# One exponential per score bank with the fp16 half copied from SBUF, and PSUM banks moved from scores to row maxima

## The chip, the cores and the metric

The kernel runs on one core of a Trainium2 chip. The metric is the device time of one execution in microseconds, from three runs of the kernel; lower is better. The engines are named as in the profile: PE (TensorE matmuls; PEld are its weight loads), DVE (VectorE), ACT (ScalarE), POOL (GpSimd) and SP (SyncE, which issues most DMAs).

## The reference

Two parts follow each other. First clustered attention: 2 batches, 8 heads, 768 tokens, head size 64. Each query and key is assigned to the nearest of 16 normalised centroids of its head, and only pairs of the same cluster may see each other:

```python
mask = q_assign[:, :, :, None] == k_assign[:, :, None, :]
scores = scale * np.matmul(q, k.transpose(0, 1, 3, 2))
scores = np.where(mask, scores, -1000000000.0)
scores = scores - np.max(scores, axis=-1, keepdims=True)
attn = np.exp(scores)
attn = attn / (np.sum(attn, axis=-1, keepdims=True) + 1e-09)
return np.matmul(attn, v).astype(np.float32)
```

Its result, as 1536 tokens of 512 values, goes through two feed-forward layers (512 to 2048 to 512), each `g(x @ w_in) @ w_out`. The first has a quadratic piece between -1 and 1 and the identity above, the second is `s * relu(h)**2 + b`. The weights arrive as float64 and are converted on the chip.

## The kernel before

The program is one hand-written order of instructions for each engine, and each engine runs its own in order. Precision comes from splitting: a number is held as a high part and a low part, and a product is three matmuls (high by high, high by low, low by high).

**Attention** is a loop over 96 slots, six for each of the 16 heads; a slot `t` handles 128 keys against all 768 queries of a head, the 768 in two halves of 384, one PSUM bank each. `slot(t)` emits, in this order: `max_mm(u, 0)` for a slot nine later (`LEAD = 9`); the DMAs planned for the slot; `scores(t)`, two matmuls into each of two banks "s"; `max_mm(u, 1)`; `finish` of a head that ended (DVE reads the bank "o"); the PE, ACT and DVE parts of planned steps; `max_reduce(u)`, two reductions on DVE that read the two banks "m"; `probs(t)`; and `values(t - 2)` (`LAG = 2`), 18 small matmuls that take `ph` and `pl` as weights and accumulate into the single bank "o".

`probs(t)` makes from each half of the scores an fp16 exponential `ph` and an fp32 exponential `pf` of the same numbers, two ACT instructions per half (L823, L824). POOL then takes the difference `pl = pf - ph` (L826; DVE does it in two slots). `pf` has two buffers, `ph` and `pl` three each.

**PSUM** has eight banks, given out from four pools, each of which hands out its banks in turn: "s" has 3, "m" 2, "o" 1, "x" 2. A pool hands a bank to its next user, and that user's first write waits until every reader of the bank's last user has finished. `spare()` takes a bank of the kind that stands next in the list `spares`, or of "x" if the list is empty.

Planned work lies between: transposes of q and k (L491, their high halves taken out of PSUM by ACT at L504), cluster assignment (L544, L583), the scaling of v (`split_v`, two ACT instructions of L673 for each pair of heads), the row that carries a head's maximum (`max_row`, L791 and a DMA `qb<-mr`), and `x_out`, the transposes of a finished pair of heads (L884), which ACT and DVE read at L889 and L892.

**Feed-forward** is 96 units. `ff_step(n)` emits `emit_h` of unit `n` (12 matmuls into one bank "h"), then `ff_rest(n)` (ACT, DVE and POOL work: the activation of unit `n`, the split of unit `n - 1`, the conversion of coming weights), then `emit_y` of unit `n - 2` (12 matmuls into four banks "y", taken from "m", "x", "o", "m"). In the first layer the bank of `h` is read last by L268 on DVE, and the conversions of weights (four DVE instructions each, L151 to L163) stand ahead of it in DVE's order. The bank of `h` comes from the pool "s".

The two parts overlap at the seam: unit 0 runs in slots 91 to 94, in a bank "m", unit 1 in slots 96 and 97, in a bank "s". From slot 98 on `spares` holds "s", so that the two `x_out` of the last pair take banks of that pool too, and the order on PE from there is: y of unit 0, `x_out(7, 0)`, h of unit 2, `x_out(7, 1)`, h of unit 3, y of unit 1, h of unit 4, y of unit 2.

```python
        for n in range(2):
            at(extra, NS + 3 + n, lambda n: whole(x_out(NP - 1, n)), n)
...
        at(extra, NS + 2, spares.append, "s")
...
        for n in range(2, TAIL):
            at(extra, NS + n + 1, emit_h, *units[n])
            at(extra, NS + n + 1, ff_rest, n)
```

Of the kernel before, what the change touches and what calls it, by code (L numbers as in the profile page):

```python
# [13 lines left out]
ACTF = mybir.ActivationFunctionType  # L14
# [11 lines left out]
def clustered_attention_moe_kernel(  # L26
# [24 lines left out]
    nc = tc.nc  # L51
# [16 lines left out]
    qk_scale = 1.0 / float(D) ** 0.5  # L68
# [26 lines left out]

    banks = {
        x: ctx.enter_context(tc.tile_pool(name="ps_" + x, bufs=n, space=PSUM))
        for x, n in (("s", 3), ("m", 2), ("o", 1), ("x", 2))
    }

    def bank(kind, name):
# [305 lines left out]
    def attention(es, prep):  # L407
# [35 lines left out]
        spares = []  # L443
# [324 lines left out]
        def max_first(i, fill):  # L768


            hd = heads[i]
            m2 = smp.tile([128, J, 2], F32, tag="rowmax2", name="rowmax2", bufs=2)
            for j in range(J):
                for n in range(2):
                    ps = spare()[:, 0:S // 2]
                    nc.tensor.matmul(
                        ps, lhsT=hd["qb"][0:NQ, j * 128:(j + 1) * 128],
                        rhs=hd["kb"][0:NQ, n * S // 2:(n + 1) * S // 2], start=True, stop=True,
                    )
                    if fill:  # L780
                        f, a, k = fill.pop(0)
                        f(*a, **k)
                    nc.vector.tensor_reduce(out=m2[:, j, n:n + 1], in_=ps, axis=AX.X, op=ALU.max)
            max_end(i, m2)
# [33 lines left out]
        def probs(t):  # L818
            pf = pp.tile([128, S], F32, tag="pf", name="pf")
            ph = phl.tile([128, S], F16, tag="ph", name="ph")  # L820
            pl = phl.tile([128, S], F16, tag="pl", name="pl")
            for qs, ps in pr[t]:
                nc.scalar.activation(out=ph[:, qs], in_=ps, func=ACTF.Exp, scale=qk_scale)  # L823
                nc.scalar.activation(out=pf[:, qs], in_=ps, func=ACTF.Exp, scale=qk_scale)  # L824
            eng = nc.vector if t in VPL else nc.gpsimd
            eng.tensor_tensor(out=pl, in0=pf, in1=ph, op=ALU.subtract)  # L826
            pr[t] = (ph, pl)
# [191 lines left out]
        def slot(t):  # L1019
            x = steps.get(t - 1, ())  # L1020
            u = t + LEAD
            has_max = 0 <= u < NS
            if has_max:
                max_mm(u, 0)
            for f, a in dmas.get(t, ()):
                f(*a)
            if 0 <= t < NS:
                scores(t)
            if has_max:
                max_mm(u, 1)  # L1030
            d = t - 1 - LAG
            if 0 <= d < NS and d % J == J - 1:
                finish(d // J)
            run(x, 3)
            if has_max:
                max_reduce(u)
            run(x, 1)
            if 0 <= t < NS:
                probs(t)
            run(x, 2)  # L1040
            for f, a in mid.get(t, ()):
                f(*a)
            if 0 <= t - LAG < NS:
                values(t - LAG)
            run(steps.get(t, ()), 0)
            for f, a in extra.get(t, ()):
                f(*a)
# [71 lines left out]
        for x in (s0, s1):  # L1119
# [5 lines left out]
            out=eye[:, 2:4], in0=ident[0:2, 0:2], scalar1=2.0 ** -14 / S, scalar2=None, op0=ALU.mult  # L1125
# [25 lines left out]
        for a in range(2):  # L1151
            for t in range(2):
                for x in sims1:
                    x[0](((a, t),), fill)
        spares[:] = ["s", "m", "s", "m", "s"]
        max_first(0, fill)
        spares[:] = ["o"]
        whole(max_row(0))
# [24 lines left out]
    with tc.manual_schedule():  # L1183
        with ExitStack() as es, ExitStack() as prep:
            attention(es, prep)
        ff_pools(("wc", NWC))
        for n in range(TAIL, len(units) + 2):
            ff_step(n)
# [33 lines left out]
```

## Time and profile before

| what | value |
|---|---|
| median of 3 runs | 767.8 us (767.29 to 767.82) |
| span of the profiled execution, first to last instruction | 766.2 us |
| PE busy, all of the span | 747.7 us (98%) |
| ACT busy | 472.9 us (62%) |
| DVE busy | 483.3 us (63%) |
| POOL busy | 318.3 us (42%) |
| mean granted TensorE clock | 0.997 of full |

The profile is of one execution and gives no total time of its own, only the span; the median of the runs is 1.6 us above that span, and what is said of microseconds of the span is carried over to the runs as it stands. PE is busy nearly throughout, so its few idle stretches are what waits show; the other engines are near their limits only in the attention loop and shortly after it.

### The profile page before, as it was taken

What the parts mean: (1) busy time and instruction counts of PE and PEld (TensorE: products, weight loads), DVE (VectorE), ACT (ScalarE), POOL (GpSimd) and SP (SyncE); (2) the same over time, 40 slices, a digit from 0 to 9 for tenths busy, and PEclk for the clock granted to TensorE, in tenths of its full rate; (3) what the DMA queues carried; (4) which work ended last, traced back from release to release, by engine and by line L of the source; (5) the groups of instructions that cost most, each with busy time, mean ns of one, the idle gap of its engine ahead of it and who ended that gap; (6) DMA issues with size and microseconds to landing.
All of it is one profiled execution on the core that took longest, in us unless ns stands there. A gap on an engine that the chain in (4) does not pass through costs nothing.

```text
span 766.2 us, 13218 instructions
## 1 busy us (share of the span) xinstructions
PE 747.7 (98%) x5019; PEld 622.5 (81%) x5019; DVE 483.3 (63%) x871; ACT 472.9 (62%) x949; POOL 318.3 (42%) x242
## 2 busy tenths in 40 slices
PE   8899999999999999999999999999999999999998
PEld 5678888988877787888888888888888888888886
DVE  6889898898887968885464349889932222222222
ACT  5389799898997777777466247866643333333332
POOL 4388688687885463555043004655630000000000
PEclk9999999999999999999999999999999999999999
DMA  9777657376511443443022003434400100010001
GB/s 199 166 154 167 142 111 174 93 162 165 134 55 58 137 138 111 137 138 111 0 84 83 0 1 119 136 103 142 133 1 1 55 1 1 0 56 1 0 1 55
DMA packets 59887, 67.52 MB, mean 88 GB/s; under 512 B 29008, under 2 KB 47536, under 8 KB 59824
## 3 DMA queue, kind: packets, MB, share of 16 engines
q1 hardware_dynamic: 59792, 66.63, 33.3%
q8 instruction: 39, 0.64, 0.4%
q14 instruction: 24, 0.20, 0.1%
q10 hardware_dynamic: 32, 0.05, 0.0%
HBM read 43.03 MB, written 3.15 MB: 60 GB/s over the span
## 4 chain that ended last, share of the span: by engine, by line
PE 83%; DVE 9%; DMA 3%; ACT 3%; issue 1%; SPq 0%; DVEq 0%; ACTq 0%
PE y L302 33%; PE h L241 32%; PE o L842 4%; PE m L747 3%; PE s L812 3%; PE s L813 3%; DVE rowmax L758 3%; PE xb L544 1%; DVE vl L677 1%; DMA rv<-in_v_dram 1%; DMA kb<-oht 1%; ACT ph L823 1%; DMA rk<-in_k_dram 1%; ACT pf L824 1%; PE xb L491 1%
## 5 line engine op out<-in xcount | busy, mean ns | idle before, releaser
L241 PE MATMUL h<-xt_h,w 128*128 128x512 f32 x768 | 252.9, 390 | 0.5 <-ACT w L179 0.4
L826 POOL TENSOR_TENSOR pl<-pf,ph 128x768 f16<-128x768 f32 x94 | 156.8, 1674 | 50.8 <-ACT pf L824 22.6
L241 PEld LDWEIGHTS h<-xt_h,w 128*128 128x128 f32 x768 | 144.1, 188 | 30.8 <-ACT w L179 0.8
L241 PE MATMUL h<-xt_l,w 128*128 128x512 f32 x384 | 149.6, 390 | 0.0
L277 POOL TENSOR_TENSOR gl<-g,gh 128x512 fp32r<-128x512 f32 x51 | 66.8, 1309 | 182.2 <-ACT gh L275 177.5
L275 ACT ACTIVATE gh<-g 128x512 fp32r<-128x512 f32 x96 | 60.4, 630 | 106.5 <-PE y L302 66.7
L823 ACT ACTIVATE ph<-s 128x384 f16<-128x384 f32 x192 | 102.1, 532 | 29.9 <-PE s L813 28.6
L302 PE MATMUL y<-gh,w 128*128 128x512 f32 x384 | 108.5, 390 | 1.2 <-DVE t L163 1.0
L758 DVE TENSOR_REDUCE rowmax<-m 128x1 f32<-128x384 f32 x180 | 95.4, 549 | 15.8 <-PE m L747 14.7
L302 PE MATMUL y<-w,gh 128*128 128x512 f32 x384 | 105.2, 389 | 0.0
L824 ACT ACTIVATE pf<-s 128x384 f32<-128x384 f32 x192 | 103.5, 539 | 0.0
L270 DVE TENSOR_SCALAR g<-g,cols 128x512 f32<-128x512 f32 x48 | 27.5, 573 | 100.8 <-ACT g L261 100.6
L302 PEld LDWEIGHTS y<-gh,w 128*128 128x128 f32 x384 | 72.0, 188 | 17.8 <-DVE t L163 1.4
L241 PEld LDWEIGHTS h<-xt_l,w 128*128 128x128 f32 x384 | 72.1, 188 | 14.9 <-DVE xt_l L892 0.2
L302 PEld LDWEIGHTS y<-w,gh 128*128 128x128 f32 x384 | 72.0, 188 | 15.0
L180 POOL TENSOR_TENSOR w<-t,w 128x512 fp32r<-128x512 f32 x64 | 83.1, 1309 | 0.0
L260 ACT ACTIVATE g<-h 128x512 f32<-128x512 f32 x48 | 28.6, 596 | 78.2 <-PE h L241 76.3
L747 PE MATMUL m<-kb,qb 80*128 80x384 f32 x180 | 68.4, 381 | 2.6 <-DVE rowmax L758 2.1
L277 DVE TENSOR_TENSOR gl<-g,gh 128x512 fp32r<-128x512 f32 x45 | 31.2, 693 | 62.5 <-ACT gh L275 62.5
L842 PEld LDWEIGHTS <-ph 128*128 128x128 f16 x1152 | 54.8, 98 | 19.0 <-issue 13.5
L812 PE MATMUL s<-qa,ka 128*128 128x384 f32 x192 | 66.7, 347 | 0.2 <-ACT pf L824 0.2
L813 PE MATMUL s<-qb,kb 128*128 128x384 f32 x192 | 65.0, 338 | 1.9 <-DMA qb<-mr 1.9
(195 smaller groups left out, 1304.4 us busy)
## 6 DMA issues: line engine op xcount, KB each, us to landing
raw<-in_moe_w_in_dram SPq DMA_DIRECT2D x32, 512.0 KB, 3.7
raw<-in_moe_w_out_dram SPq DMA_DIRECT2D x32, 512.0 KB, 3.3
rq<-in_q_dram SPq DMA_DIRECT2D x16, 192.0 KB, 4.4
rk<-in_k_dram SPq DMA_DIRECT2D x16, 192.0 KB, 4.9
rv<-in_v_dram SPq DMA_DIRECT2D x8, 384.0 KB, 5.3
out_dram<-o SPq DMA_DIRECT2D x12, 256.0 KB, 2.3
qb<-qh SPq DMA_DIRECT2D x14, 192.0 KB, 3.2
kb<-kh SPq DMA_DIRECT2D x14, 192.0 KB, 3.8
```

The source lines that it names most:

```text
L180: nc.gpsimd.tensor_tensor(out=l, in0=f, in1=h.bitcast(F32), op=ALU.subtract)
L241: nc.tensor.matmul(h_t[m, t, c], lhsT=w[:, kk * 128:(kk + 1) * 128], rhs=x[:, kk, tokens(t)], start=((n, kk) == H_PARTS[0]), stop=((n, kk) ...
L277: eng.tensor_tensor(out=gl, in0=g, in1=gh.bitcast(F32), op=ALU.subtract)
L302: nc.tensor.matmul(y[i], lhsT=ops[n][0], rhs=ops[n][1], start=(begin and n == 0), stop=(end and n == 2))
L747: nc.tensor.matmul(ps, lhsT=hd["qb"][0:NQ, j * 128:(j + 1) * 128], rhs=hd["kb"][0:NQ, n * S // 2:(n + 1) * S // 2], start=True, stop=True,)
L758: nc.vector.tensor_reduce(out=hd["m2"][:, j, n:n + 1], in_=mst.pop((u, n)), axis=AX.X, op=ALU.max)
L812: nc.tensor.matmul(ps, lhsT=hd["ka"][:, cs], rhs=hd["qa"][:, qs], start=True, stop=False)
L813: nc.tensor.matmul(ps, lhsT=hd["kb"][:, cs], rhs=hd["qb"][:, qs], start=False, stop=True)
L823: nc.scalar.activation(out=ph[:, qs], in_=ps, func=ACTF.Exp, scale=qk_scale)
L824: nc.scalar.activation(out=pf[:, qs], in_=ps, func=ACTF.Exp, scale=qk_scale)
L826: eng.tensor_tensor(out=pl, in0=pf, in1=ph, op=ALU.subtract)
L842: nc.tensor.matmul(o[:, j, 0:w], lhsT=lhsT[:, js], rhs=rhs[:, e, c, :], start=(c == 0 and j == 0 and x == 0), stop=(c == J - 1 and j == J ...
```

## The change

Scores get two PSUM banks in place of three and row maxima three in place of two. `probs` takes one exponential per half, in fp32, and makes the fp16 half by one ACT copy of all 768 columns from `pf` in SBUF, once both exponentials are there. The list of spare banks for the first head's maxima is adapted to the new counts.

```diff
-        for x, n in (("s", 3), ("m", 2), ("o", 1), ("x", 2))
+        for x, n in (("s", 2), ("m", 3), ("o", 1), ("x", 2))
...
             for qs, ps in pr[t]:
-                nc.scalar.activation(out=ph[:, qs], in_=ps, func=ACTF.Exp, scale=qk_scale)
                 nc.scalar.activation(out=pf[:, qs], in_=ps, func=ACTF.Exp, scale=qk_scale)
+            nc.scalar.activation(out=ph, in_=pf, func=ACTF.Copy)
             eng = nc.vector if t in VPL else nc.gpsimd
             eng.tensor_tensor(out=pl, in0=pf, in1=ph, op=ALU.subtract)
...
-        spares[:] = ["s", "m", "s", "m", "s"]
+        spares[:] = ["m", "s", "m", "s", "m"]
         max_first(0, fill)
```

## Rows read from the trace of the kernel before

**Rows 1.** The page, POOL's costliest group: busy us, mean ns | idle before, releaser.

```profile
L826 POOL TENSOR_TENSOR pl<-pf,ph 128x768 f16<-128x768 f32 x94 | 156.8, 1674 | 50.8 <-ACT pf L824 22.6
```

**Rows 2.** Busy time by stretch: PE, PEld, DVE, ACT, POOL, then clock, DMA, GB/s.

```profile
40.00:240.00 200.00, 192.88 (x2543) 168.71 (x2542) 171.24 (x373) 176.94 (x450) 157.84 (x103) 1.00 0.57 131
...
300.00:766.00 466.00, 462.46 (x2041) 382.59 (x2039) 231.91 (x353) 233.24 (x384) 113.77 (x89) 1.00 0.18 58
```

**Rows 3.** Waits of PE's weight loads, 40 to 240 us: total, times, longest.

```profile
PEld L842 <- DVE x L860: 4.7, 11, 0.8
PEld m L747 <- DVE rowmax L758: 4.1, 11, 0.8
...
PEld s L812 <- ACT pf L824: 1.2, 4, 0.5
```

**Rows 4.** Timeline of ACT, slots 33 to 35: start, us, instruction.

```profile
107.16 0.49 ACT L823 ACTIVATE ph<-s 128x384 f16<-128x384 f32 x1 [0.52 <-PE s L813]
...
108.65 0.64 ACT L673 ACTIVATE vh<-rv,sc 128x384 f16<-128x384 f32 x1
109.16 0.51 ACT L823 ACTIVATE ph<-s 128x384 f16<-128x384 f32 x1
...
111.63 0.56 ACT L823 ACTIVATE ph<-s 128x384 f16<-128x384 f32 x1
112.00 0.57 ACT L824 ACTIVATE pf<-s 128x384 f32<-128x384 f32 x1
```

**Rows 5.** Timeline of PE, the four score matmuls of slot 36 (two shown).

```profile
112.22 0.34 PE L812 MATMUL s<-qa,ka 128*128 128x384 f32 x1
...
112.62 0.44 PE L812 MATMUL s<-qa,ka 128*128 128x384 f32 x1
```

**Rows 6.** Timeline of ACT: a copy from SBUF and the next start, then a dependent pair.

```profile
238.83 0.61 ACT L179 ACTIVATE w<-t 128x512 fp32r<-128x512 f32 x1
239.35 0.26 ACT L867 ACTIVATE xb<-rowmax,cols 128x12 f32<-128x12 f32 x1
...
247.96 0.69 ACT L256 ACTIVATE g<-h,cols 128x512 f32<-128x512 f32 x1 [1.21 <-PE h L241]
248.68 0.72 ACT L257 ACTIVATE g<-g,cols 128x512 f32<-128x512 f32 x1
```

**Rows 7.** Timeline of ACT, the start of slot 90's exponentials.

```profile
225.40 0.65 ACT L823 ACTIVATE ph<-s 128x384 f16<-128x384 f32 x1
```

**Rows 8.** Timeline of PE: the first score matmul of slot 91.

```profile
225.68 0.42 PE L812 MATMUL s<-qa,ka 128*128 128x384 f32 x1
```

**Rows 9.** Timeline of PE at the seam, the first matmul of each piece.

```profile
244.48 0.60 PE L884 MATMUL sb<-ident,x 128*128 128x128 f32 x4
244.83 0.47 PE L241 MATMUL h<-xt_h,w 128*128 128x512 f32 x1
...
247.90 0.47 PE L241 MATMUL h<-xt_h,w 128*128 128x512 f32 x1
...
250.74 0.39 PE L302 MATMUL y<-gh,w 128*128 128x512 f32 x1
...
254.04 0.50 PE L241 MATMUL h<-xt_h,w 128*128 128x512 f32 x1 [0.42 <-ACT w L179]
...
257.62 0.50 PE L302 MATMUL y<-gh,w 128*128 128x512 f32 x1 [0.22 <-ACT part L327]
```

**Rows 10.** Timeline of DVE at the seam: the last reads of two "h" banks.

```profile
244.60 0.69 DVE L268 TENSOR_TENSOR g<-g,h 128x512 f32<-128x512 f32 x1
...
252.13 0.68 DVE L268 TENSOR_TENSOR g<-g,h 128x512 f32<-128x512 f32 x1
```

**Rows 11.** Timeline of DVE: the last read of unit 45's "h" bank.

```profile
487.98 0.68 DVE L268 TENSOR_TENSOR g<-g,h 128x512 f32<-128x512 f32 x1
```

**Rows 12.** Timeline of PE: y of unit 44, then h of unit 47.

```profile
487.58 1.07 PE L302 MATMUL y<-gh,w 128*128 128x512 f32 x4
...
490.30 0.39 PE L241 MATMUL h<-xt_h,w 128*128 128x512 f32 x1
```

## The prediction

> **What bounds the kernel now.** I read the busy times by stretch first [rows 2]: from 40 to 240 us, the attention loop, PE is busy 192.9 of 200 us and ACT 176.9; from 300 us on PE is busy 462 of 466 and ACT half. So PE sets the pace throughout, and a change can only take away waits of PE or add some. Then the waits of PE's weight loads in the loop [rows 3], which show better than the modelled matmul ends where PE stood still: 4.1 us for row-maximum banks that DVE had not yet read (11 times), 4.7 us at `finish`, only 1.2 us for score banks that ACT had not yet read. Last the order of time at the seam, where a pool of three "s" banks becomes one of two while four kinds of users pass through it.
>
> **Row maxima, 2 banks to 3.** With two, the first `max_mm` of a slot waits for the first reduction of the slot before; with three it waits for one a reduction older, half a slot earlier. The 4.1 us [rows 3] are the most that this stretch can give. Where DVE is behind for longer than one bank covers, PE only arrives earlier at the `finish` of the head, whose 4.7 us of waits on DVE [rows 3] then grow. Bounds 2.0 (half of it comes back there) and 4.1; the waits are short (0.8 at most) and eleven against 180 reductions, so DVE catches up between most of them: I take 3.5 saved.
>
> **ACT's work per slot.** Before: four exponentials, 0.37 us apart (112.00 after 111.63 [rows 4]), so 4 x 0.37 = 1.48 us until ACT is free. After: an exponential (0.37), a second one, and a copy that reads what the second wrote. A dependent instruction starts only when the other has ended: 0.72 us after the start of one that lasts 0.69 [rows 6], where an instruction of the same width that depends on nothing is followed after 0.52 (238.83 to 239.35 [rows 6]). So the second exponential, 0.51 long, holds the copy back for 0.53. The trace has no ACT instruction of 768 columns. From below it is two of 384, 2 x 0.37 = 0.74; from above 384 columns cost 0.37 and 512 from SBUF 0.52, 0.15 for 128 more, and 256 more make 0.82. I take 0.75, near the lower end, because the 512 columns carried over in proportion make 0.78 and a part of each instruction is fixed. Sum 0.37 + 0.53 + 0.75 = 1.65, that is 0.17 more a slot, although one instruction fewer is issued. Bounds: 0.37 + 0.37 + 0.74 = 1.48 (no drain, no change) and 0.37 + 0.57 + 0.82 = 1.76 (0.28 more).
>
> The trace speaks here against a rule that the change would live by. The Trainium skill, "Advanced Engine Details and Errata", section The Read-Write Bubble, says that on ScalarE the latency of the memories shows between instructions and not within one, so fewer and larger ones should be cheaper; with the figures of "ScalarE: Activation LUTs", section What ACT_TABLE_LOAD costs (186 ns + 0.833 ns a column, 93 ns overlapped), my estimate is four times 413 ns before against 2 x 413 + 733 ns after, 0.09 us saved a slot. By these ACT would lose nothing in the loop and the attention part would come out some 2 us shorter than I say; the dependent pair in the rows shows a drain that the estimate has not.
>
> **Scores, 3 banks to 2.** Before, the first half of slot t+1 needs the bank of slot t-1's second half, and the second half the bank of slot t's first, which was free after ACT's second instruction. Now both halves need the banks of slot t, free after ACT's first and second instruction. In a plain slot that costs nothing: ACT starts 0.55 us after the scores (107.16), and one exponential has ended by 107.65 [rows 4], while the next scores come a good second later. It costs where ACT is late. Slot 33 starts freely [rows 4], then two `split_v` and a transpose keep ACT back to back until slot 35's exponentials at 111.63. With 0.17 more in each of the two slots these start at 111.97; the first ends 0.57 later, at 112.54; PE follows a release by 0.05 (112.00 + 0.57 = 112.57, and the waiting matmul at 112.62 [rows 4, 5]): 112.59, where slot 36 started at 112.22 [rows 5]. That is 0.37 us of PE. The pattern comes once per pair of heads, seven times in the loop; two of them fall before long PE work, so I take 0.3 each, 2.1 together. In slots 89 to 91 ACT is later still: slot 90's exponentials start at 225.40 and last 0.65 [rows 7], so slot 91 can start at 226.10, not at 225.68 [rows 8]: 0.4 even at unchanged speed. Sum 2.5 lost. From below 0.4 (ACT's slot unchanged); from above 0.28 a slot, which is 26 us over 94 slots, more than ACT's 23 idle us [rows 2]: 0.6 at seven places, 0.4, and the 3 us that don't fit, 7 in all.
>
> POOL's `pl` starts some 0.1 us later a slot. It takes 1.67 us [rows 1] and its `values` come two slots later; `pf` is now written by ACT's first instruction and not the second, so it waits for the `pl` of two slots before 0.37 earlier. Two plain slots of 1.73 us leave just about the time for both; this may cost a tenth in some slots and is inside the upper bound. The new order of spare banks names the same five banks for the first head's maxima, hidden behind DVE's reductions; without that cover it is one reduction, 0.5 us.
>
> **The seam.** This is where I expect most. The users of "s" after slot 95's two halves are h of unit 1, `x_out(7, 0)`, h of unit 2, `x_out(7, 1)`, h of unit 3. With three banks they get the third, first, second, third and first: unit 3 gets the bank of `x_out(7, 0)`, long read. With two they alternate, and unit 3 gets the bank of unit 2, two users back. That bank is read last by L268 at 252.13, for 0.68 us, behind eight conversion instructions on DVE [rows 10]; unit 3 started at 247.90 [rows 9]. So PE waits from 247.90 until 252.81 + 0.05 = 252.86: 4.96 us. Nothing can pass it: y of unit 1 stands behind it on PE. (Unit 2 too gets the bank of unit 1, read until 245.29 [rows 10] against 244.83 [rows 9]: 0.5 us, which lies ahead of the same DVE chain and adds nothing.)
>
> Some comes back. Before, h of unit 4 waited for weights and y of unit 2 for copies of the finished y [rows 9], and both will be ready: from 252.86, h of unit 3 takes 2.84 (247.90 to 250.74 [rows 9]), then y of unit 1 and h of unit 4 2.72 each (as a y late in the layer, 487.58 to 490.30 [rows 12]): y of unit 2 at 261.14, against 257.62 [rows 9]. Net 3.5 lost. Bounds 2.0 (DVE gets through its conversions earlier, or later waits vanish as well) and 5.0 (nothing is given back). Afterwards two banks alternate between units and are enough: even in a late, tight unit the bank is read by 488.66 [rows 11] and wanted at 490.30 [rows 12].
>
> **Sum.** -3.5 + 2.5 + 3.5 = +2.5 us on a span whose median run is 767.8: 770.3.
>
> **Rivals.** *No change* (767.8): the copy follows the exponential without a drain and ACT's slot stays 1.48, so that score banks cost only 0.4; -3.5 + 0.4 + 3.5 = +0.4, within 1.5 us (0.2%, about what this kernel's measurement tells from nothing). For it: independent ACT instructions overlap by a quarter of their length [rows 4]. Against: the dependent pair [rows 6]. By the rule of the Trainium skill in "Advanced Engine Details and Errata", The Read-Write Bubble, this is the case to expect. *Faster* (766.8): unit 3 doesn't get a bank whose reader is late, because the pool hands banks out in another order or DVE is through before 247.95; the seam then costs nothing and the rest gives -1.0, with the no-drain case -3.1. It decides from 247.95, the end of L268. For it: no row shows an "s" bank's number. Against: slot 36's second score matmul waits for slot 35's first exponentials [rows 4, 5], which is taking turns. *ACT becomes the bound* (774.8): 0.28 a slot, loss 7; -3.5 + 7 + 3.5 = +7. For it: 176.9 of 200 us busy [rows 2]. Against: it needs both upper ends at once.
>
> **Numbers.** Forecast 0.5, of which 0.07 ends within 0.2%; no change 0.2, nearly all within; faster 0.15, of which 0.03 within and the rest below; ACT bound 0.15. So faster by over 0.2%: 0.15, within 0.27, slower 0.58. The likeliest time is 770.3, its own range 768.3 to 772.8. The range for 8 in 10 takes in the no-change case, the shallower half of the faster one and the nearer part of the ACT-bound one: 766.3 to 774.3.
>
> **What would show it.** PE's waits on row-maximum banks nearly gone and those on score banks at 2 to 3 us, at the slots after two `split_v`. A copy of 768 columns of about 0.85 us, its start just behind the end of the second exponential. At the seam one PE wait of h (L241) for L268 of 4 to 5 us, right after the second `x_out`, and none for weights behind it. The prediction is wrong if that wait is missing, if the copy starts before the exponential ends, or if the DVE waits reappear in full at `finish`.

## The result, and the profile after

The changed kernel takes 775.73 us (median; 775.25 to 776.75) against 767.81 (767.29 to 768.78): ratio 1.0098, 95% interval 1.0080 to 1.0117. That is 7.9 us slower where 2.5 were forecast, and outside the range of 766.3 to 774.3. The profiled execution has a span of 774.1 us, 7.9 above that of before.

From the page, PE's group that has a new wait, then groups of POOL and ACT:

```profile
L241 PE MATMUL h<-xt_h,w 128*128 128x512 f32 x768 | 254.5, 392 | 5.5 <-DVE g L268 4.5
L826 POOL TENSOR_TENSOR pl<-pf,ph 128x768 f16<-128x768 f32 x94 | 156.2, 1665 | 53.5 <-ACT ph L824 35.9
...
L823 ACT ACTIVATE pf<-s 128x384 f32<-128x384 f32 x192 | 82.9, 484 | 26.0 <-PE s L813 23.6
...
L824 ACT ACTIVATE ph<-pf 128x768 f16<-128x768 f32 x96 | 81.1, 844 | 3.0
```

The waits of PE's weight loads from 40 to 240 us, against [rows 3]:

```profile
PEld L842 <- DVE x L860: 4.6, 11, 0.8
PEld s L812 <- ACT pf L823: 3.8, 10, 0.6
...
PEld m L747 <- DVE rowmax L758: 1.6, 3, 1.3
PEld L842 <- POOL pl L826: 1.1, 5, 0.3
PEld h L241 <- ACT pf L823: 1.1, 1, 1.1
```

PE at the seam, the first matmul of each piece, against [rows 9], and the last read of unit 2's bank on DVE, against [rows 10]:

```profile
246.74 0.60 PE L884 MATMUL sb<-ident,x 128*128 128x128 f32 x4
247.61 0.50 PE L241 MATMUL h<-xt_h,w 128*128 128x512 f32 x1 [0.27 <-DVE g L268]
...
250.46 0.38 PE L884 MATMUL sb<-ident,x 128*128 128x128 f32 x2
255.11 0.80 PE L241 MATMUL h<-xt_h,w 128*128 128x512 f32 x1 [4.27 <-DVE g L268]
255.71 0.63 PE L241 MATMUL h<-xt_l,w 128*128 128x512 f32 x1
...
260.24 0.40 PE L302 MATMUL y<-gh,w 128*128 128x512 f32 x1
...
265.69 0.39 PE L302 MATMUL y<-gh,w 128*128 128x512 f32 x1
```

```profile
254.38 0.68 DVE L268 TENSOR_TENSOR g<-g,h 128x512 f32<-128x512 f32 x1
```

The same place by stretch (columns as in [rows 2]; the granted clock stands before the DMA share): PE's work before, the wait, h of unit 3, and the work behind it:

```profile
245.00:250.50 5.50, 5.21 (x25) 3.90 (x24) 4.85 (x8) 2.03 (x4) 1.94 (x2) 1.00 0.31 98
250.90:255.10 4.20, 0.00 (x0) 0.00 (x0) 3.99 (x7) 2.63 (x6) 0.20 (x1) 0.77 0.39 125
255.10:260.20 5.10, 5.09 (x12) 4.02 (x13) 2.98 (x5) 1.67 (x3) 3.76 (x3) 0.52 0.50 156
260.20:265.60 5.40, 5.40 (x25) 4.45 (x24) 2.98 (x5) 4.61 (x8) 0.86 (x1) 1.00 0.12 47
```

Two things are to be seen in these. The wait that the prediction placed is there, behind the second `sb` and for L268, 4.27 us. And the twelve matmuls after it run at half the granted clock (0.52, the 1.2 GHz level), 0.43 us apart in place of 0.23; h of unit 3 takes 255.11 to 260.24, 5.13 us, where before it took 2.84 [rows 9].

Where the 7.9 us came from is read from the starts of the same matmuls in both profiles, as a shift (after less before):

| point on PE | before | after | shift | added since |
|---|---|---|---|---|
| slot 14, first score matmul | 63.13 | 63.34 | +0.21 | 0.21 |
| slot 95, first score matmul | 234.94 | 236.55 | +1.61 | 1.40 |
| y of unit 0 | 241.14 | 243.41 | +2.27 | 0.66 |
| h of unit 3 | 247.90 | 255.11 | +7.22 | 4.95 |
| y of unit 1 | 250.74 | 260.24 | +9.50 | 2.28 |
| y of unit 2 | 257.62 | 265.69 | +8.07 | -1.43 |
| h of unit 95 | 751.42 | 759.33 | +7.91 | -0.16 |

### The profile page after: what moved, and what is told of

Same layout as the page of the kernel before. It is cut to its first block, busy times and chain, and to the rows that moved or that the text cites. A ratio compares the mean times of both kernels' runs of the same rounds, so it can differ in the third digit from the quotient of the medians.

```text
span 774.1 us, 13215 instructions
## 1 busy us (share of the span) xinstructions
PE 750.3 (97%) x5019; PEld 624.2 (81%) x5019; DVE 483.6 (62%) x871; ACT 478.2 (62%) x853; POOL 317.5 (41%) x242
## 4 chain that ended last, share of the span: by engine, by line
PE 83%; DVE 6%; ACT 4%; DMA 3%; issue 2%; SPq 1%; POOL 1%; ACTq 0%; DVEq 0%; POOLq 0%
PE y L302 33%; PE h L241 33%; PE o L842 4%; PE s L812 3%; PE m L747 3%; PE s L813 3%; ACT pf L823 2%; DVE rowmax L758 1%; PE xb L544 1%; DMA rk<-in_k_dram 1%; SPq L460 1%; DMA rv<-in_v_dram 1%; ACT ph L824 1%; PE xb L491 0%; POOL pl L826 0%
## 5 line engine op out<-in xcount | busy, mean ns | idle before, releaser
L823 ACT ACTIVATE pf<-s 128x384 f32<-128x384 f32 x192 | 82.9, 484 | 26.0 <-PE s L813 23.6
L824 ACT ACTIVATE ph<-pf 128x768 f16<-128x768 f32 x96 | 81.1, 844 | 3.0
```

The lines of the kernel that those rows point to most:

```text
L824: nc.scalar.activation(out=ph, in_=pf, func=ACTF.Copy)
```

## The experiments

Three batches, each on one chip with runs of the kernel before: 767.93 us in the first, 768.06 in the second, 768.61 in the third. What a run showed is given as its median and, from its one profiled execution, as shifts against the kernel before: "loop" from slot 14 to slot 95, "tail" from there to y of unit 0, "wait" from there to h of unit 3, "h" from there to y of unit 1. What lies ahead of slot 14 is in none of these columns. They were worked out in the same way as in the table above, from rows that aren't shown.

| kernel | median us | ratio, 95% interval | loop | tail | wait | h |
|---|---|---|---|---|---|---|
| changed kernel | 775.73 | 1.0098 (1.0080 to 1.0117) | +1.40 | +0.66 | +4.95 | +2.28 |
| the same again | 774.96 | 1.0075 (1.0060 to 1.0090) | -0.11 | +0.67 | +4.95 | +1.61 |
| banks alone | 778.39 | 1.0133 (1.0118 to 1.0149) | +4.44 | +0.13 | +4.81 | +1.60 |
| exponential and copy alone | 771.00 | 1.0053 (1.0030 to 1.0076) | +2.66 | +0.94 | +0.01 | -0.01 |
| second transpose in "m" | 769.79 | 1.0022 (1.0006 to 1.0038) | +0.07 | +0.68 | +0.48 | +0.01 |
| and h of unit 1 in "m" | 769.90 | 1.0021 (1.0002 to 1.0040) | +0.42 | +0.68 | 0.00 | -0.03 |
| and copy in halves | 770.24 | 1.0019 (1.0006 to 1.0031) | -0.81 | +0.58 | -0.02 | 0.00 |
| idle matmuls in the wait | 775.41 | 1.0093 (1.0058 to 1.0128) | +4.66 | +0.69 | +4.95 | +0.01 |
| the same again | 773.45 | 1.0055 (1.0041 to 1.0069) | +0.34 | +0.67 | +4.96 | +0.05 |
| halves, filled slot 6 | 768.50 | 0.9990 (0.9972 to 1.0009) | -1.15 | +0.49 | -0.01 | -0.02 |
| one copy, filled slot 6 | 767.96 | 0.9995 (0.9981 to 1.0009) | -0.17 | +0.70 | -0.01 | -0.01 |
| before, filled slot 6 | 767.88 | 0.9988 (0.9976 to 1.0000) | -0.25 | -0.01 | +0.01 | 0.00 |
| halves, banks of before | 773.53 | 1.0054 (1.0032 to 1.0075) | +1.37 | +0.51 | -0.02 | -0.02 |

**Banks alone,** against the changed kernel: the copy goes and the fp16 exponential of each half comes back.

```diff
+                nc.scalar.activation(out=ph[:, qs], in_=ps, func=ACTF.Exp, scale=qk_scale)
...
-            nc.scalar.activation(out=ph, in_=pf, func=ACTF.Copy)
```

> The bank counts of the change with the four exponentials of before. Theory (the seam costs through the bank of unit 2's h and through the TensorE clock that falls after the wait, the copy costs in the attention loop): the seam's wait of some 4.4 us before h of unit 3 and h of unit 3 at half clock stay, some 5 us in all, while the loop is no slower than before: 771.5 to 773.5 us. Rival (two score banks cost in the loop, the copy nothing): 774.5 to 776 us.

778.39 bears out neither: it is slower than the whole change. The seam cost what it cost there, but the loop lost 4.4 us, which the theory had left with the copy. PE's weight loads from 40 to 240 us:

```profile
PEld s L812 <- ACT pf L824: 15.1, 50, 0.5
```

With two banks the next slot's halves wait for the last readers of this slot's. With four exponentials these are ACT's second and fourth instruction of the slot, with one per bank its first and second. So the single exponential is what makes two score banks bearable. I had worked the waits out for the two edits together only.

**Exponential and copy alone,** against the changed kernel.

```diff
-        for x, n in (("s", 2), ("m", 3), ("o", 1), ("x", 2))
+        for x, n in (("s", 3), ("m", 2), ("o", 1), ("x", 2))
...
-        spares[:] = ["m", "s", "m", "s", "m"]
+        spares[:] = ["s", "m", "s", "m", "s"]
```

> One exponential and the copy with the three score banks and two maxima banks of before. Theory: no wait before h of unit 3 and full clock there; ACT's slot is 0.16 us longer and PE's waits on maxima banks stay as before: the loop 0.5 to 2.5 us longer, 768.3 to 770.3 us. Rival (the copy costs nothing, or the shorter chain of instructions gains): 767.8 us or less.

The wait at the seam and the slow h are gone, as the theory has it; the loop lost 2.7 us and the tail 0.9, and the time, 771.00, is above its 770.3. PE's waits for maxima banks stay, those for score banks shrink:

```profile
PEld m L747 <- DVE rowmax L758: 5.0, 10, 1.0
...
PEld s L812 <- ACT pf L823: 0.6, 1, 0.6
```

The waits for maxima banks (5.0 against 4.1) and new ones for `pl` (0.6) add 1.5 and those for score banks give 0.6 back; the rest of the 2.7 was not traced. So in the profiles, with the copy in place, the bank trade is worth some 2.8 us of the loop (2.66 against -0.11 in the repeated profile of the change), and the two edits together cost the loop about nothing where no late DMA is in it. The medians show less: 771.00 against 769.79 for both edits with the seam mended, the next run, on the same chip.

**The second transpose in a maxima bank.**

```diff
-        at(extra, NS + 2, spares.append, "s")
+        at(extra, NS + 2, spares.extend, ["s", "m"])
```

> The changed kernel, with the second transpose of the last pair in a maxima bank, so that h of unit 3 gets the bank of the first one, long read. Theory: the 4.4 us wait goes and with it the fall of the clock; what the waits gave back (1.6 us) is no longer given back: 775.7 - 5.1 = 770.6 us. Rival (another wait of the seam, weights or DVE's conversions, takes its place): above 773 us.

The theory's way: 769.79, a little below its 770.6. h of unit 3 no longer waits and runs at full clock; nothing took the wait's place. Of the 7.9 us that the change cost over the kernel before, 1.9 are left (769.79 against 767.93).

**h of unit 1 in a maxima bank too.**

```diff
-                ff["h"] = bank("ms"[n], "h")
+                ff["h"] = bank("mm"[n], "h")
```

> The changed kernel with the second transpose in a maxima bank, as in the run before, and h of unit 1 in a maxima bank too, so that it no longer waits for slot 95's first exponential. Theory: the 1.0 us wait of h of unit 1 goes, but slot 95's pl still sets when values and y of unit 0 can end, so of the 1.0 us some 0 to 0.7 is gained: 769 to 769.8 us. Rival (that wait is simply added time): 1.2 us gained, 768.6 us.

The tail is 0.68 in both profiles. The 1.0 us wait of h of unit 1 for slot 95's first exponential went, but PE then waits for `pl` there, 0.4 and 0.6 us, as the theory has it. Only the 0.48 of "wait", which is h of unit 2 behind unit 1's bank, was gained in the profile. The medians (769.9 and 769.8) don't tell the two kernels apart.

**Idle matmuls inside the wait,** against the changed kernel. `warm(18, "m")` emits 18 matmuls into a bank "m" whose result nobody reads; `NS` is 96, the number of slots.

```diff
+        at(extra, NS + 4, lambda: warm(18, "m"))
```

> The changed kernel, with 18 idle matmuls of 512 columns into a free maxima bank between the second transpose and h of unit 3, some 3.9 us of PE work inside the 4.3 us wait. They add work whose result nobody reads. Theory (the wait itself is not shortened, but PE's clock falls because PE stood still): h of unit 3 starts when it did and takes 2.8 us in place of 5.1, 775.7 - 2.3 = 773.4 us. Rival (the slow matmuls have another cause, for instance their operands or the memory): no change, 775.7 us, or later by the added work.

Inconclusive as a time: its runs lay from 772.04 to 778.62, and the profiled one, the slowest, lost 4.7 us in the loop, nearly all of it in slots 66 and 67 behind late DMAs (one wait of PE of 3.19 us for `qb<-mr`), with a granted clock of 0.66 from 182 to 187 us. Its h of unit 3 ran at full clock, so it was run again, with the changed kernel beside it.

> The changed kernel with 18 idle matmuls inside the seam's wait once more, beside the changed kernel itself on the same chip. Theory (the clock at half after the wait costs 2.3 us): its fast runs 2 to 2.5 us below those of the changed kernel. Rival (no cost of the clock): within 0.5 us of it.

> The changed kernel as it is, on the chip of these runs: 775.7 us as before. It shows how far the DMA waits of the loop (rv, qb<-mr) differ from one profiled execution to the next: by the theory the waits on banks repeat to 0.3 us and the DMA waits do not.

773.45 against 774.96, 1.5 us less, below the 2 to 2.5 expected, near the 1.6 that h of unit 3 had lost in the profile of the changed kernel beside it, and off the rival's none. By stretch, the filled wait and the h behind it, where the changed kernel's second row has PE idle:

```profile
250.30:254.90 4.60, 4.24 (x22) 1.84 (x20) 4.36 (x8) 2.91 (x6) 0.57 (x1) 1.00 0.38 114
254.90:257.80 2.90, 2.90 (x13) 2.36 (x14) 2.73 (x5) 1.63 (x3) 2.19 (x2) 1.00 0.58 181
```

The shift of the wait is as large (4.96 against 4.95) and h takes 2.89 us in place of 5.13 or, in the repeated profile, 4.46. So the slow matmuls come from PE having stood still and from nothing in their operands. The repeat of the changed kernel also shows the spread: its profiled run, the fastest of its six (772.86), had the loop at -0.11 against +1.40. Of these 1.5 us 1.3 lie in one wait for a maxima bank at 178.8 (the 1.3 in the table of waits above), behind a reduction on DVE that waited for the values' DMA:

```profile
177.33 0.95 DVE L618 TENSOR_REDUCE ab<-rv 128x2 f32<-128x768 f32 x1 [2.17 <-DMA rv<-in_v_dram]
```

The expectation that waits on banks repeat and DMA waits don't held for the score banks, 3.8 us in both profiles. For maxima banks it did not: 1.6 us against 0.4, since a late DMA shows up there as a wait on a bank. What made that DMA late in one execution is not shown.

**The copy in halves,** with both seam edits.

```diff
-            nc.scalar.activation(out=ph, in_=pf, func=ACTF.Copy)
+            for qs, ps in pr[t]:
+                nc.scalar.activation(out=ph[:, qs], in_=pf[:, qs], func=ACTF.Copy)
```

> As the kernel with both seam edits, but the copy is made in two halves of 384, so that the first half depends on an exponential that has already ended and no drain of 0.15 us stands in the slot. Four ACT instructions again, about 0.37 + 0.37 + 0.41 + 0.41 = 1.56 us in place of 1.64. Theory (the drain is what makes ACT late): waits of PE on score banks and on pl shrink by half, some 1 to 1.5 us gained against the kernel with one copy, about 768 us. Rival (fewer, larger instructions are cheaper, so four are dearer than three): 0.5 to 2 us lost, 770 to 771 us.

In the profile the loop is 1.2 us shorter than with one copy (-0.81 against +0.42), in the middle of the theory's figure, but the medians are 770.2 and 769.9: no gain in time is shown. Up to slot 14 this profile is 1.31 us behind the kernel before, more than the loop gains. The two stretches around the wait of slot 6 show where:

```profile
42.00:46.30 4.30, 2.08 (x26) 1.55 (x24) 3.28 (x6) 2.45 (x6) 4.05 (x3) 1.00 0.80 177
46.30:52.00 5.70, 5.66 (x61) 5.08 (x61) 2.45 (x7) 3.66 (x9) 2.27 (x3) 0.70 0.93 198
```

PE stood still for 2.26 us there, for the DMA that brings the second head's maxima row, and the clock fell to 0.70 in the mean of what followed. From the end of that wait to slot 7's first score matmul PE takes 2.82 us here, 2.99 with one copy, where the clock fell too, and 1.64 in the kernel before, whose clock stayed at 1.00: the fall costs 1.2 to 1.35 us up to there. The length of the wait does not decide by itself. It was 1.70 in the kernel before; 1.72 in the kernel with the second transpose in "m" was followed by the fall (0.71 from 46.3 to 52 us), and 2.46 in the first run with idle matmuls at the seam was not (1.00). The kernel with one copy is 1.10 behind at slot 14, so this does not say why the medians of the two are alike.

**Slot 6 filled** with seven idle matmuls (`J` is 6), in three kernels: with the halves, with one copy, and in the kernel before.

```diff
                 nc.tensor.matmul(ps, lhsT=hd["ka"][:, cs], rhs=hd["qa"][:, qs], start=True, stop=False)
+                if t == J and n == 0:
+                    warm(7, "m")
```

> The kernel with both seam edits and the copy in two halves, with seven idle matmuls in slot 6 behind the first score matmul, where PE waits for a DMA (the maxima row of the second head) and where the clock had fallen in three profiles. They add work whose result nobody reads. Theory (the fall of the clock after that wait is what keeps the kernel above the one before): its median falls by 1 to 2 us, to 768 to 769 us, level with the kernel before or below it. Rival (the loop itself is slower by ACT): no change, 770 us.

> Both seam edits, one copy of 768 columns, and the seven idle matmuls in slot 6. Theory: 0.5 to 1.2 us above the same kernel with the copy in halves, since ACT's slot is 0.08 us longer; 768.5 to 769.7 us. Rival (one copy is cheaper): below the one with halves.

> The control: the kernel before with the same seven idle matmuls in slot 6. Theory: its runs at a granted clock of 0.995 (769 to 770 us) become fewer, its median moves from 768 to 767.2 to 768 us. Rival (the matmuls only add work): 768.5 us or more.

768.50 and 767.96, 1.7 and 1.9 us less than without the fill on another chip; the kernel before took 768.61 here, and both are level with it by their intervals. From 46.3 to 52 us the granted clock is 1.00 in all three filled kernels, and 0.70 to 0.73 in the three seam-mended ones without the fill. The control moved to 767.88, 0.7 less. In the one profile without the fill its clock there was 1.00 already, but its executions at a mean clock of 0.995 or less went from 10 of 30 to 1 of 12, as its theory has it. What the changed kernels gain beyond that 0.7 fits the 1.2 to 1.35 us of the fall, but it is not shown to be that alone: with one copy the mean clock of the twelve executions rose from 0.9955 to 0.9980, with the halves only from 0.9955 to 0.9962. No version is shown to beat the kernel before. Between halves and one copy the profile (-1.15 and -0.17 in the loop) and the medians (0.5 us the other way) disagree once more, and that stays open.

**Halves with the bank counts of before.** The kernel before, with one exponential per half and the two half copies of above.

> One exponential and the copy in two halves with the bank counts of before (three for scores, two for maxima) and the seam of before. Theory: the waits on maxima banks stay (some 5 us of weight loads), those on score banks and pl are small: 769 to 770 us, 1 to 2 us under the kernel with one copy and these counts. Rival (the three banks hide the copy's drain, so halves bring nothing): 771 us.

The loop is 1.3 us shorter than with one copy and these counts (+1.37 against +2.66), but the time is 773.5, above the rival's 771: the profiled run was 4.35 us behind already at slot 14. Of these 0.74 are older than slot 6, 1.16 are a longer wait on the same DMA (2.86 against 1.70), and 2.45 come in the stretch behind it, where the clock fell to 0.65 from 46.3 to 52 us. What made that wait longer here was not tried, so neither figure is tested.

## Why the prediction was wrong

Two steps failed, by about as much. Up to y of unit 0 the forecast was -3.5 + 2.5 = -1.0 and the profile of the result has +2.27; for the seam it was +3.5 and that profile has +5.64. The medians divide the 7.9 us in a like way: about 6.1 went with the seam's wait and 1.9 stayed, of which a part lies in slot 6, ahead of the loop.

**The seam, place and length: right.** h of unit 3 waited for unit 2's bank. The shift between y of unit 0 and h of unit 3 is 4.95 us, forecast 4.96, and 4.95 again in the second profile. Taking the second transpose out of the pool removed it.

**The seam, price: the first step that failed.** "From 252.86, h of unit 3 takes 2.84" took the length of h from a stretch in which PE had not stood still. It took 5.13 us in the one profile and 4.46 in the other, so the net 3.5 became 5.80 and 5.15 at y of unit 2 (wait, h and what came back: 4.95 + 2.28 - 1.43 in the first, 4.95 + 1.61 - 1.41 in the second, whose y of unit 2 stands at +5.15). The upper bound of 5.0 was set by "nothing is given back" and had no term for the clock. The 1.43 that came back is the forecast 1.44. The profile of before has no wait of this length in the loop or at the seam, but it does have a fall of the clock, which the prediction does not use, early on, where PE is idle in pieces, 3.3 of 20 us (the clock is the last number but two):

```profile
20.00:40.00 20.00, 16.70 (x93) 13.73 (x94) 16.50 (x38) 8.88 (x23) 6.96 (x6) 0.91 0.79 171
```

The Trainium skill, "TensorE: Matmul & The Clock Gate", Part 1 on the clock gate, says that PE's clock halves when it has been idle and comes back when it has been busy; this case's rows agree (0.52 after the wait, 1.00 with the wait filled), and by that rule the seam's term would have been about 2 us larger.

**ACT's slot: right.** The copy starts 0.02 us behind the end of the second exponential, and three consecutive rows give the slot (the first holds both exponentials):

```profile
109.41 0.85 ACT L823 ACTIVATE pf<-s 128x384 f32<-128x384 f32 x2
110.28 0.84 ACT L824 ACTIVATE ph<-pf 128x768 f16<-128x768 f32 x1
111.04 0.60 ACT L673 ACTIVATE vh<-rv,sc 128x384 f16<-128x384 f32 x1
```

Two exponentials take 0.87 (109.41 to 110.28) and the copy holds ACT for 0.76 more: 1.63, forecast 1.65. No version here shows ACT getting cheaper with three instructions than with four. In the loop's shifts one copy is dearer than two half copies in all three pairs of profiles (by 1.0 to 1.3 us); the medians don't show it.

**Maxima and score banks: right in size.** PE's waits on maxima banks fell from 4.1 us to 1.6, or 0.4 in the second profile: 2.5 to 3.7 saved, forecast 3.5. Waits on score banks rose from 1.2 to 3.8: 2.6, forecast 2.5. Slot 36's first score matmul shows it, after a slot 35 whose exponentials start at 112.02:

```profile
112.55 0.44 PE L812 MATMUL s<-qa,ka 128*128 128x384 f32 x1
```

It stands at +0.33, of which 0.03 is older (slot 35); forecast +0.37, and 0.3 as the mean.

**What the loop's sum left out: the second step that failed.** Two terms stood at nothing: values that wait for `pl`, 1.1 and 1.0 us in the two profiles of the changed kernel (put inside the upper bound and not in the sum), and the tail, 0.66 and 0.67. With the waits as measured, the loop comes out as -2.5 + 2.6 + 1.1 = +1.2 in the first profile, whose shift is +1.40, and -3.7 + 2.6 + 1.0 = -0.1 in the second, whose shift is -0.11. The waits of the second, 40 to 240 us:

```profile
PEld s L812 <- ACT pf L823: 3.8, 10, 0.6
...
PEld L842 <- POOL pl L826: 1.0, 4, 0.3
...
PEld m L747 <- DVE rowmax L758: 0.4, 2, 0.2
```

The tail is 0.13 with the banks alone and 0.94 with the copy alone, so it comes with the copy: slots 94 and 95 have ACT as their pace, and y of unit 0 waits for what they produce. ACT itself waits there, in slot 94, for `pl` of two slots before, the wait on `pf` that I had named and priced at a tenth:

```profile
235.73 0.87 ACT L823 ACTIVATE pf<-s 128x384 f32<-128x384 f32 x2 [0.49 <-POOL pl L826]
```

From slot 14 to y of unit 0 the profiles have +2.06 and +0.56 against the forecast -1.0. So the step was short by 1.6 in the better of two executions, about what `pl` and the tail make. The other adds 1.5, most of it the wait at 178.8 behind a DMA, which no term of mine covered. A further 0.8 between the two stands already at slot 14; its cause is not traced.

**Rivals.** The faster one fell with the wait at the seam. The unchanged one fell with ACT's slot: 1.63 us and not 1.48, and waits on score banks up by 2.6 and not 0.4. ACT as the bound is not the cause either: it needs 7 us of waits on score banks, the loop cost 1.4 and -0.1, and the time that this rival gives, 774.8, is near by chance. (Its 7 is a slip: 0.6 at seven places, 0.4 and 3 make 7.6. And the seam's wait turns on 247.85, not 247.95, since PE follows a release by 0.05. Neither changes the argument.) None of the three things that were to show the prediction wrong was seen: the mechanisms that it named were there, and what failed were prices: that of the seam's wait and those that it put at nothing.

## What to carry to other kernels

When a pool loses a buffer, list its users in order across the stage borders, not only in the loop that the count was chosen for: here one stray user turned the rotation so that a matmul met a bank two users back. A long wait on PE is priced at its length and at the slower matmuls that may follow it. And two edits that touch one resource are to be costed separately as well: in the profiles the bank trade alone cost the loop 4.4 us, the copy alone 2.7, both together between -0.2 and +0.4 in five of seven; the other two (1.4 and 4.7) met a late DMA in slot 66.

## What the runs showed of the hardware

A wait of PE of 4.27 us was followed by 12 matmuls of 512 columns at 0.43 us each in place of 0.23; with idle matmuls in the wait they came 0.24 apart. Granted clock and time went together in the changed kernel's six runs on the second chip: 772.9 us at a mean clock of 0.996, 774.9 to 775.0 at 0.993 and 775.3 to 775.4 at 0.991. They need not: the kernel before has two runs of 770.3 at 1.000 on the third chip, where its median is 768.6. Also unexpected: in slot 6 waits of 1.72 and 2.26 us on PE were followed by the lower clock, and ones of 1.70 and 2.46 were not.
